# A two-pass channel-attention kernel: the last loads and the maxima back at one width, the first reload cut into six pieces and taken from its last rows, the reloads issued in written order

## The chip, the cores and the metric

The kernel runs on one core of a Trainium2 chip. The metric is the device time of one execution in microseconds.

## The reference

`x` is an image of 384 x 384 positions with 384 channels in bf16 (113 MB), `w1` is 384 x 96 and `w2` is 96 x 384. The mean and the maximum of each channel over all positions go through the same two small matrix products; the sum, through a sigmoid, scales each channel of `x`.

```python
xf  = x.reshape(B, H * W, C)
gap = jnp.mean(xf, 1)
gmp = jnp.amax(xf, 1)
h_a = relu(gap @ w1)
h_m = relu(gmp @ w1)
scale = sigmoid(h_a @ w2 + h_m @ w2)
return x * scale[:, None, None, :]
```

No output element can be written before all of `x` has been read once. The data does not fit in on-chip memory, so most of it is read a second time.

## The kernel before, in words

**Rows and blocks.** The 147456 positions are laid on 128 partitions, 1152 "rows" of 384 channels each. A row over all partitions is 98304 bytes. The first 16 rows are copied to PSUM (`kept_ps`) and stay there; the next 10 rows are read into their own place and read again later into `acc`; the other 1126 rows form 26 blocks: block 0 has 26 rows, blocks 1 to 25 have 44. Six buffers of 44 rows (`slots`, called x_79 to x_84 in the profile, slot 0 to slot 5) take them in turn, so that the last six blocks, 20 to 25, sit in slots 0 to 5 when the first pass ends.

**First pass.** Each entry of `loads` is one DMA on SyncE's queue (L167). For each, TensorE adds the rows to the channel sums (L134), and VectorE takes the maximum of `acc` (11 rows) with up to `width` of the entry's rows at a time (L180). `LAST_LOADS` says into how many pieces the last 13 blocks are cut; all earlier blocks are one DMA of 44 rows. Ahead of the last eight loads, `fold` (L157) takes the maximum of `acc`'s rows 8 to 10 into its first three, and from there on the maxima are 8 rows wide (`NARROW`). The last two loads (`SUM_TAIL`) get their sums through other matmuls (L151), after the earlier sums were turned round in `turn_sums` (L145, L146).

**Between the passes.** VectorE folds `acc` from 8 rows to 1 (L157). Behind the first and the last fold, the rows of `acc` that are free are reloaded with `x` (L201). TensorE transposes the one row left (L204), VectorE reduces it (L205), the two products follow (L207, L209), and ScalarE writes the scale (L210).

**Second pass.** `put` multiplies a block's rows in place, piece by piece, on VectorE (L215), and issues one store per piece on ScalarE's queue (L233); `put_acc` (L222) does so with `acc` after the third piece of the first block. `FIRST_STORES` cuts the first three blocks into pieces; later blocks are one piece. `get` issues the reloads of blocks 0 to 19 on SyncE's queue (L244). After two blocks (`LEAD`) have been put, the first two reloads are written into the program, first the one into slot 1, then the one into slot 0, each in two pieces of 22 rows (`FIRST_READS`); from then on one reload of one piece follows each block, into the slot that the block left. The list `order`, to which each reload is appended, gives the order of the later multiplications. At the end the rows kept in PSUM are multiplied into a slot and stored (L274).

**What sets the order.** The kernel writes no semaphores. A scheduler in the compiler takes the program, keeps the data dependences down to the rows concerned, and may order an engine's instructions otherwise than they are written. A reload waits for the stores of the rows that it overwrites. An engine's queue is in order: a DMA that waits holds back the later ones of its queue.

Of the kernel before, what the change touches and what calls it, by code (L numbers as in the profile page):

```python
# [9 lines left out]
ALU = mybir.AluOpType  # L10
# [7 lines left out]
PSUM_ROWS = 16  # L18
ACC_ROWS = 11

LAST_LOADS = ((22, 22),) * 8 + ((6, 19, 19),) + ((11, 11, 11, 11),) * 2 + ((10, 10, 9, 8, 7), (8, 8, 7, 7, 7, 7))

NARROW = (8, 8)

FIRST_STORES = ((1, 2, 3, 4, 4, 6, 8, 8, 8), (8, 8, 9, 9, 10), (10, 12, 22))

FIRST_READS = (2, 2)
LEAD = 2

ACC_STORES_AT = 3  # L30
# [5 lines left out]
def kernel(  # L36
# [7 lines left out]
    nc = tc.nc  # L44
# [5 lines left out]
    A = ACC_ROWS  # L50
# [7 lines left out]
    def rows_of(ap, first, n):  # L58

        return ap[first * P:(first + n) * P, :].rearrange("(p n) c -> p n c", n=n)  # L60
# [10 lines left out]
    while left > 0:  # L71
        n = min(SLOTS[slot], left)
# [29 lines left out]
    acc = consts.tile([P, A, C], BF16)  # L102
# [17 lines left out]
    for i, (first, n, s) in enumerate(blocks):  # L120
        left = n
        for m in LAST_LOADS[i - n_blocks] if i >= n_blocks - len(LAST_LOADS) else (n,):
            m = min(m, left)
# [3 lines left out]
    n_loads = len(loads)  # L127
    tail_rows = sum(hi - lo for *_, lo, hi in loads[n_loads - SUM_TAIL:])

    def sums(rows, n, done, total):  # L130
        for k in range(0, n, MM_ROWS):
            g = min(MM_ROWS, n - k)
            for q in range(CQ):
                nc.tensor.matmul(  # L134
                    sum_ps[q * QP:q * QP + 1, 0:g * P],
                    lhsT=ones_bf[:, 0:1],
                    rhs=rows[:, k:k + g, q * P:(q + 1) * P],
                    start=(done + k == 0),
                    stop=(done + k + g == total),
                )  # L140

    def turn_sums():

        for r in range(MM_ROWS):
            nc.scalar.copy(out=s_sb[r % 2], in_=sum_ps[:, r * P:(r + 1) * P])  # L145
            nc.tensor.matmul(gsum_ps, lhsT=s_sb[r % 2], rhs=pick, start=(r == 0), stop=False)  # L146

    def tail_sums(rows, n, last):
        for k in range(n):
            for q in range(CQ):  # L150
                nc.tensor.matmul(  # L151
                    gsum_ps[:, q:q + 1], lhsT=rows[:, k, q * P:(q + 1) * P], rhs=ones_bf,
                    start=False, stop=(last and k == n - 1 and q == CQ - 1),
                )

    def fold(n, h):
        nc.vector.tensor_tensor(out=acc[:, 0:h, :], in0=acc[:, 0:h, :], in1=acc[:, n - h:n, :], op=ALU.max)  # L157

    done = 0
    width = A  # L160
    for i, (first, n, s, lo, hi) in enumerate(loads):
        if i == n_loads - NARROW[1]:
            fold(A, A - NARROW[0])
            width = NARROW[0]
        rows = slots[s][:, lo:hi, :]
        m = hi - lo
        nc.sync.dma_start(out=rows, in_=rows_of(xr, first, n)[:, lo:hi, :])  # L167
        if i < n_loads - SUM_TAIL:
            sums(rows, m, done, TOT - tail_rows)
        else:  # L170
            tail_sums(rows, m, i == n_loads - 1)
        done += m
        if i == n_loads - SUM_TAIL - 1:
            turn_sums()
        if i == 0:
            nc.vector.tensor_copy(out=acc, in_=rows[:, 0:A, :])  # L176
            lo = A
        for j in range(0 if i else A, m, width):
            k = min(width, m - j)
            nc.vector.tensor_tensor(out=acc[:, 0:k, :], in0=acc[:, 0:k, :], in1=rows[:, j:j + k, :], op=ALU.max)  # L180
        if i == 0:
            nc.vector.tensor_copy(out=kept_ps.bitcast(U32), in_=rows.bitcast(U32))  # L182
# [6 lines left out]
        nc.tensor.matmul(hTa_ps, lhsT=w1_sb[:, q, :], rhs=gT[:, q, 0:1], start=(q == 0), stop=(q == CQ - 1))  # L189
    nc.scalar.activation(out=hid[:, 0:1], in_=hTa_ps, func=ACT.Relu)  # L190
    nc.tensor.matmul(z_ps, lhsT=hid[:, 0:1].to_broadcast([R, P]), rhs=w2_sb, start=True, stop=False)
    n = width
    acc_pieces = []
    while n > 1:
        h = n // 2
        fold(n, h)
        n -= h
        if n > 1 and acc_pieces:
            continue
        lo, hi = n, acc_pieces[0][0] if acc_pieces else A  # L200
        nc.sync.dma_start(out=acc[:, lo:hi, :], in_=rows_of(xr, PSUM_ROWS, A - 1)[:, lo - 1:hi - 1, :])  # L201
        acc_pieces.append((lo, hi))
# [21 lines left out]
    def put(block, pieces, acc_at=None):  # L224

        first, n, s = block
        j = 0
        for i, m in enumerate(pieces):
            if i == acc_at:
                put_acc()  # L230
            rows = slots[s][:, j:j + m, :]
            multiply(rows, rows)
            nc.scalar.dma_start(out=rows_of(orr, first, n)[:, j:j + m, :], in_=rows)  # L233
            j += m
        assert j == n

    def cut(n, parts):
        return [n // parts + (k < n % parts) for k in range(parts)]

    def get(block, pieces):  # L240
        first, n, s = block
        j = 0
        for m in pieces:
            nc.sync.dma_start(out=slots[s][:, j:j + m, :], in_=rows_of(xr, first, n)[:, j:j + m, :])  # L244
            j += m


    order = blocks[n_stream:]
    again = sorted(blocks[:n_stream], key=lambda b: -b[1])
    stores, reads = list(FIRST_STORES), list(FIRST_READS)  # L250

    def read_into(s):
        fits = [b for b in again if b[1] <= SLOTS[s]]
        if fits:
            b = fits[0]
            again.remove(b)
            b = (b[0], b[1], s)
            get(b, cut(b[1], reads.pop(0) if reads else 1))
            order.append(b)

    k = 0
    while k < len(order):
        put(order[k], stores.pop(0) if stores else (order[k][1],), None if k else ACC_STORES_AT)
        k += 1
        if k == LEAD:
            read_into(order[k - 1][2])
            for j in range(k - 1):
                read_into(order[j][2])
        elif k > LEAD:
            read_into(order[k - 1][2])  # L270
    assert not again
    s = order[-NS][2]
    multiply(slots[s][:, 0:PSUM_ROWS, :], kept_ps)
# [29 lines left out]
```

## Time and profile before

| | |
|---|---|
| median of three runs | 746.55 us (746.23 to 748.59) |
| the profiled execution's own time | 748.59 us |
| its span, first to last instruction | 746.8 us |
| VectorE busy | 489.1 us (65%) |
| TensorE busy | 126.5 us (17%) |
| read from HBM, written to it | 199.11 MB, 113.25 MB |
| mean rate over the span | 418 GB/s |

The profiled execution is the slowest of the three and lies 2.0 us over the median; its span lies 1.8 us under its own time. Times inside the execution are given in us from the start of the span. Reads go over the queue q1 (SyncE), stores over q10 (ScalarE); both are served by the same 16 DMA engines. In the slices of the page one digit or number stands for a fortieth of the span, 18.7 us.

### The profile page before, as it was taken

To read this page: it belongs to the slowest core of one execution; us is meant where nothing else is said; L and a number is where in the kernel's file an instruction comes from. 1 tells how busy PE (TensorE), PEld (TensorE's weight loads), DVE (VectorE), ACT (ScalarE), POOL (GpSimd) and SP (SyncE) were. 2 spreads that over 40 slices of the span, in tenths; PEclk is the share of its full clock that TensorE was granted. 3 is DMA by queue.
4 is the path that set the end of the run, shared out by engine and by line. 5 is a ranking of instruction groups with operands and counts; after the bars stand their busy time and mean duration, and the time that the engine had idled before them with its cause. 6 is when DMAs were issued, how large, how long until landed. Compare 5 with 4: busy or idle time off the path is not lost.

```text
span 746.8 us, 2450 instructions
## 1 busy us (share of the span) xinstructions
PE 126.5 (17%) x958; PEld 40.3 (5%) x958; DVE 489.1 (65%) x166; ACT 3.3 (0%) x9; POOL 0.7 (0%) x6
## 2 busy tenths in 40 slices
PE   3344444445545540000000000000000000000000
PEld 0111111111111120000000000000000000000000
DVE  6789999999999989999443333444444444444600
ACT  0000000000000000000000000000000000000000
POOL 0000000000000000000000000000000000000000
PEclk9656666755555555555555555555555555555555
DMA  9999999999999959999999999999999999999996
GB/s 381 433 432 433 430 427 434 419 426 429 426 424 419 416 217 371 416 434 430 434 429 429 434 433 434 434 433 434 434 434 434 431 434 433 433 434 428 438 431 283
DMA packets 17803, 312.52 MB, mean 418 GB/s; under 512 B 2336, under 2 KB 2688, under 8 KB 6528
## 3 DMA queue, kind: packets, MB, share of 16 engines
q1 hardware_dynamic: 11600, 199.12, 62.7%
q10 hardware_dynamic: 6192, 113.25, 35.5%
q8 instruction: 7, 0.11, 0.1%
q14 instruction: 4, 0.03, 0.0%
HBM read 199.11 MB, written 113.25 MB: 418 GB/s over the span
## 4 chain that ended last, share of the span: by engine, by line
another core or an unknown queue 40%; DVE 31%; DMA 21%; DVEq 1%; issue 1%; SPq 1%; PE 0%; ACT 0%; ACTq 0%
DVE acc L180 28%; DMA out_dram<-x_83 7%; DMA x_81<-in_x_dram 6%; DMA x_79<-in_x_dram 4%; DMA out_dram<-x_80 2%; DMA x_80<-in_x_dram 2%; DVE x_79 L215 1%; DVEq L298 1%; SPq L244 1%; DVE x_80 L215 1%; DVE acc L157 0%; DVE acc L215 0%; DVE acc L176 0%; DVE kept_ps L182 0%
## 5 line engine op out<-in xcount | busy, mean ns | idle before, releaser
L215 DVE TENSOR_TENSOR x_80<-x_80,scale_bc 128x16896 bf16<-128x16896 bf16 (+3 forms) x9 | 45.1, 5044 | 34.3 <-DMA x_80<-in_x_dram 34.3
L215 DVE TENSOR_TENSOR x_79<-x_79,scale_bc 128x3072 bf16<-128x3072 bf16 (+7 forms) x13 | 41.8, 3261 | 30.5 <-DMA x_79<-in_x_dram 29.3
L215 DVE TENSOR_TENSOR x_82<-x_82,scale_bc 128x16896 bf16<-128x16896 bf16 x4 | 35.8, 8956 | 33.7 <-DMA x_82<-in_x_dram 33.7
L215 DVE TENSOR_TENSOR x_83<-x_83,scale_bc 128x16896 bf16<-128x16896 bf16 x4 | 35.8, 8957 | 33.6 <-DMA x_83<-in_x_dram 33.6
L215 DVE TENSOR_TENSOR x_84<-x_84,scale_bc 128x16896 bf16<-128x16896 bf16 x4 | 35.8, 8956 | 33.3 <-DMA x_84<-in_x_dram 33.3
L215 DVE TENSOR_TENSOR x_81<-x_81,scale_bc 128x16896 bf16<-128x16896 bf16 (+3 forms) x6 | 36.0, 6021 | 32.7 <-DMA x_81<-in_x_dram 22.0
L180 DVE TENSOR_TENSOR acc<-acc,x_84 128x4224 bf16<-128x4224 bf16 (+2 forms) x22 | 47.5, 2158 | 5.4 <-DMA x_84<-in_x_dram 4.8
L134 PEld LDWEIGHTS <-small 128*1 128x1 bf16 x897 | 36.1, 110 | 230.4 <-issue 227.2
L180 DVE TENSOR_TENSOR acc<-acc,x_83 128x4224 bf16<-128x4224 bf16 (+5 forms) x20 | 43.6, 2178 | 2.2 <-DMA x_83<-in_x_dram 1.6
L180 DVE TENSOR_TENSOR acc<-acc,x_80 128x4224 bf16<-128x4224 bf16 (+3 forms) x18 | 40.0, 2225 | 3.1 <-DMA x_80<-in_x_dram 2.5
L180 DVE TENSOR_TENSOR acc<-acc,x_79 128x4224 bf16<-128x4224 bf16 (+1 forms) x17 | 38.9, 2287 | 1.5 <-DMA x_79<-in_x_dram 1.0
L180 DVE TENSOR_TENSOR acc<-acc,x_81 128x4224 bf16<-128x4224 bf16 x16 | 37.7, 2359 | 1.9 <-DMA x_81<-in_x_dram 1.4
L180 DVE TENSOR_TENSOR acc<-acc,x_82 128x4224 bf16<-128x4224 bf16 x16 | 37.7, 2359 | 1.0 <-DMA x_82<-in_x_dram 0.5
L134 PE MATMUL bank_a<-x_83,small 128*1 128x512 bf16 (+3 forms) x162 | 22.3, 577 | 25.7 <-DMA x_83<-in_x_dram 25.7
L134 PE MATMUL bank_a<-x_79,small 128*1 128x512 bf16 (+1 forms) x150 | 20.6, 585 | 30.2 <-DMA x_79<-in_x_dram 30.2
L134 PE MATMUL bank_a<-x_80,small 128*1 128x512 bf16 (+2 forms) x147 | 20.8, 593 | 23.2 <-DMA x_80<-in_x_dram 23.2
L134 PE MATMUL bank_a<-x_84,small 128*1 128x512 bf16 (+2 forms) x162 | 20.2, 528 | 25.4 <-DMA x_84<-in_x_dram 25.4
L134 PE MATMUL bank_a<-x_82,small 128*1 128x512 bf16 (+2 forms) x138 | 18.9, 576 | 21.7 <-DMA x_82<-in_x_dram 21.7
L134 PE MATMUL bank_a<-x_81,small 128*1 128x512 bf16 (+2 forms) x138 | 18.7, 571 | 20.0 <-DMA x_81<-in_x_dram 20.0
L176 DVE COPY acc<-x_79 128x4224 bf16<-128x4224 bf16 x1 | 1.3, 1260 | 5.5 <-DMA x_79<-in_x_dram 5.5
L182 DVE COPY kept_ps<-x_79 128x3072 uint32<-128x3072 uint32 x1 | 3.4, 3355 | 0.0
L215 DVE TENSOR_TENSOR x_81<-kept_ps,scale_bc 128x6144 bf16<-128x6144 bf16 x1 | 3.4, 3352 | 0.0
(37 smaller groups left out, 21.0 us busy)
## 6 DMA issues: line engine op xcount, KB each, us to landing
x_84<-in_x_dram SPq DMA_DIRECT2D x5, 4224.0 KB, 30.0
x_80<-in_x_dram SPq DMA_DIRECT2D x5, 4224.0 KB, 30.5
x_81<-in_x_dram SPq DMA_DIRECT2D x5, 4224.0 KB, 30.2
x_82<-in_x_dram SPq DMA_DIRECT2D x5, 4224.0 KB, 30.0
x_83<-in_x_dram SPq DMA_DIRECT2D x5, 4224.0 KB, 30.4
x_79<-in_x_dram SPq DMA_DIRECT2D x4, 4224.0 KB, 30.2
out_dram<-x_82 ACTq DMA_DIRECT2D x4, 4224.0 KB, 75.3
out_dram<-x_83 ACTq DMA_DIRECT2D x4, 4224.0 KB, 70.8
```

Of the source, the lines that this page charges most:

```text
L134: nc.tensor.matmul(sum_ps[q * QP:q * QP + 1, 0:g * P], lhsT=ones_bf[:, 0:1], rhs=rows[:, k:k + g, q * P:(q + 1) * P], start=(done + k == 0 ...
L176: nc.vector.tensor_copy(out=acc, in_=rows[:, 0:A, :])
L180: nc.vector.tensor_tensor(out=acc[:, 0:k, :], in0=acc[:, 0:k, :], in1=rows[:, j:j + k, :], op=ALU.max)
L182: nc.vector.tensor_copy(out=kept_ps.bitcast(U32), in_=rows.bitcast(U32))
L215: nc.vector.tensor_tensor(out=dst, in0=src, in1=scale_bc.unsqueeze(1).to_broadcast([P, n, C]), op=ALU.mult)
L244: nc.sync.dma_start(out=slots[s][:, j:j + m, :], in_=rows_of(xr, first, n)[:, j:j + m, :])
L298: with _tile.TileContext(nc) as tc:
```

## The change

Three things change together.

1. The first pass. The last 12 blocks (before: 13) are cut, eight into two loads of 22 rows and four into four of 11. Before, block 21 was cut into 6, 19 and 19 rows, block 24 into five and block 25 into six pieces. `NARROW` and the fold ahead of the last eight loads go; the maxima stay 11 rows wide, and the last folds go from 11 rows (5, 3, 1, 1 rows) instead of from 8 (4, 2, 1).
2. The first reloads. The reload into slot 0 is written ahead of that into slot 1. It is cut into six pieces of 4, 4, 6, 8, 10 and 12 rows instead of two of 22; the one into slot 1 stays at two of 22. `get` now begins with a block's last rows and goes back to its first.
3. The order. All of the second pass stands in a block in which SyncE's instructions are issued as written.

```diff
-LAST_LOADS = ((22, 22),) * 8 + ((6, 19, 19),) + ((11, 11, 11, 11),) * 2 + ((10, 10, 9, 8, 7), (8, 8, 7, 7, 7, 7))
-
-NARROW = (8, 8)
+LAST_LOADS = ((22, 22),) * 8 + ((11, 11, 11, 11),) * 4
...
-FIRST_READS = (2, 2)
+FIRST_READS = ((4, 4, 6, 8, 10, 12), (22, 22))
...
-        if i == n_loads - NARROW[1]:
-            fold(A, A - NARROW[0])
-            width = NARROW[0]
...
-        for j in range(0 if i else A, m, width):
-            k = min(width, m - j)
+        for j in range(0 if i else A, m, A):
+            k = min(A, m - j)
...
-    n = width
+    n = A
...
     def get(block, pieces):
         first, n, s = block
-        j = 0
+        j = n
         for m in pieces:
+            j -= m
             nc.sync.dma_start(out=slots[s][:, j:j + m, :], in_=rows_of(xr, first, n)[:, j:j + m, :])
-            j += m
+        assert j == 0
...
-            get(b, cut(b[1], reads.pop(0) if reads else 1))
+            get(b, reads.pop(0) if reads else (b[1],))
             order.append(b)
...
+    in_order = ctx.enter_context(ExitStack())
+    in_order.enter_context(tc.manual_schedule(engines={mybir.EngineType.SP}))
     k = 0
     while k < len(order):
...
         if k == LEAD:
-            read_into(order[k - 1][2])
-            for j in range(k - 1):
+            for j in range(k):
                 read_into(order[j][2])
         elif k > LEAD:
             read_into(order[k - 1][2])
+    in_order.close()
```

More of the change, by code (lines that the diff above doesn't have):

```diff
@@ L154, in tail_sums @@
                 )
-    def fold(n, h):
-        nc.vector.tensor_tensor(out=acc[:, 0:h, :], in0=acc[:, 0:h, :], in1=acc[:, n - h:n, :], op=ALU.max)
     done = 0
-    width = A
     for i, (first, n, s, lo, hi) in enumerate(loads):
-        if i == n_loads - NARROW[1]:
-            fold(A, A - NARROW[0])
-            width = NARROW[0]
         rows = slots[s][:, lo:hi, :]
@@ L195 @@
         h = n // 2
-        fold(n, h)
+        nc.vector.tensor_tensor(out=acc[:, 0:h, :], in0=acc[:, 0:h, :], in1=acc[:, n - h:n, :], op=ALU.max)
         n -= h
@@ L235, in put @@
         assert j == n
-    def cut(n, parts):
-        return [n // parts + (k < n % parts) for k in range(parts)]
     def get(block, pieces):
         first, n, s = block
-        j = 0
+        j = n
         for m in pieces:
+            j -= m
             nc.sync.dma_start(out=slots[s][:, j:j + m, :], in_=rows_of(xr, first, n)[:, j:j + m, :])
-            j += m
+        assert j == 0
     order = blocks[n_stream:]
```

## The prediction

> **What bounds the kernel now.** First the page's slices, to see which resource is full where.
>
> ```profile
> DVE  6789999999999989999443333444444444444600
> DMA  9999999999999959999999999999999999999996
> GB/s 381 433 432 433 430 427 434 419 426 429 426 424 419 416 217 371 416 434 430 434 429 429 434 433 434 434 433 434 434 434 434 431 434 433 433 434 428 438 431 283
> ```
>
> DMA is full except at the start, at slice 15 (261 to 280 us), where the first pass ends and the scale is made, and in the last slice. After 400 us VectorE is busy for 134.37 of 300 us and the rate is a flat 433 GB/s. So the time is the bytes over that rate, plus three holes. The change touches the middle hole and the DMAs just behind it.
>
> What makes the middle hole shows in the timeline (start, us, engine, line, tile).
>
> ```profile
> 137.45 4.75 DVE L180 TENSOR_TENSOR acc<-acc,x_83 128x4224 bf16<-128x4224 bf16 x2 [0.50 <-DMA x_83<-in_x_dram]
> ...
> 263.08 9.92 DVE L180 TENSOR_TENSOR acc<-acc,x_84 128x3072 bf16<-128x3072 bf16 x6
> 273.04 1.95 DVE L157 TENSOR_TENSOR acc<-acc 128x1536 bf16<-128x1536 bf16 x3
> ...
> 290.21 9.81 SPq L244 DMA_DIRECT2D x_79<-in_x_dram  x2
> ...
> 312.59 5.29 SPq L244 DMA_DIRECT2D x_80<-in_x_dram  x2
> ```
>
> VectorE last waits for a load at 137.45, for block 12, which comes as one DMA of 44 rows. From there to 275.00 it runs without a gap. The loads' last packets end by 270 (the window 268 to 270 moved 73 GB/s), so VectorE, not the load, opens the hole. TensorE is through with the averages at 272.47, 2.5 us before it is needed. The same view shows SyncE issuing x_79's reload ahead of x_80's although the program has them the other way: the scheduler already had that order.
>
> Behind the hole I asked for the busy time by stretch (last columns: DMA share, GB/s).
>
> ```profile
> 282.00:290.00 8.00, 0.00 (x0) 0.00 (x0) 8.00 (x7) 0.00 (x0) 0.00 (x0) 0.50 1.02 407
> 290.00:300.00 10.00, 0.00 (x0) 0.00 (x0) 10.00 (x6) 0.00 (x0) 0.00 (x0) 0.50 1.00 356
> 300.00:312.00 12.00, 0.00 (x0) 0.00 (x0) 12.00 (x4) 0.00 (x0) 0.00 (x0) 0.50 1.01 426
> 740.00:746.80 6.80, 0.00 (x0) 0.00 (x0) 0.00 (x0) 0.00 (x0) 0.00 (x0) 0.50 0.15 64
> ```
>
> While x_79's first reload mixes with the first block's last stores the engines are busy but move 356 GB/s: against 433 that loses 10 x (1 - 356/433) = 1.8 us. And at the end 6.8 us move 0.44 MB, 1.0 us of work: the 16 engines finish unevenly, and 5.8 us go to waiting for the last.
>
> **What the Trainium skill says.** "DMA: Bandwidth & Descriptors", Queues, rings and completion order: SyncE and ScalarE own a ring each on the same 16 engines, which take turns between them by packets. The trace agrees: from 600 to 700 us q1 had 46.2% and q10 53.8% of the time. Same page, Anatomy of one DMA: about 2 us of a DMA are fixed, mostly the receipt at the end; here a 96 KB store took 1.7 us to landing. Same page, Where 436 GB/s comes from: a ceiling of 435 GB/s; here 433. "VectorE: DVE Perf Modes", Mode 2x_1P: two bf16 results a cycle, so 384 elements at its 0.96 GHz are 200 ns, an estimate. The groups by form say 2358 ns for 4224 elements and 359 for 384: 200 a row, and 159 fixed.
>
> **The change part by part.**
>
> *Start of the chain.* Block 13 becomes one load. VectorE ended block 12 at 147.02 and took block 13's first half at once; now it waits for the whole block. Whole blocks came 10.03 apart (waits that end at 107.36 and 137.45), so 137.45 + 10.03 = 147.48: **+0.46**.
>
> *The maxima.* Before, from 147.02 to 273.04: 126.02, with pieces of 6 to 10 rows and one extra fold. After: 13 blocks of four 11-row maxima, 9.57 a block (127.41 and 137.0 bracket one): 124.41, **-1.61**. The maxima end at 271.89.
>
> *Does the last load hold them up?* Matmuls on 11-row pieces start 2.57 apart (233.57, 236.14, 238.70). Block 21 ends at 228.44; sixteen pieces more give 228.44 + 41.1 = 269.5. The last maximum wants to start at 271.89 - 2.39 = 269.50. A tie: I take 0; if the loads are late, this gain shrinks.
>
> *The folds.* Before 4, 2, 1 rows: 0.96 + 0.56 + 0.36 with gaps, 1.96. After 5, 3, 1, 1: 1.16 + 0.76 + 0.36 + 0.36 + gaps = 2.70: **+0.74**. So `acc` is down to one row at 274.59 instead of 275.00: **-0.41** for the scale and all behind it, since transposes to sigmoid (275.04 to 277.93) stay.
>
> *Hidden there.* The last two loads have 22 rows instead of 14: 66 tail matmuls for 42, at 30 ns (1.26 us for 42) 0.7 us. TensorE's chain then ends near 269.5 + 1.0 + 1.7 = 272.2, under the folds' end by 2.4. `turn_sums` and the two weight loads on SyncE come earlier, since the third last load does. `acc` reloads 5 + 5 rows for 7 + 3: the second piece, issued at 274.6, carries 0.2 MB more, 0.5 us, and lands near 278.8; its multiplication starts at about 280.1 (three pieces and five rows after 277.5). Covered by 1.3 us; without the cover, at most 0.5.
>
> *The reload into x_79.* Its first piece now overwrites rows 40 to 43 and waits for that slot's last store, issued at 289.64 - 0.4 = 289.2; its sisters took 4.2 to land: about 293.4, where before the first half went at 290.2 and the second at 299.7. Four more DMAs at 0.33 to 0.42 on SyncE, 1.5 us; behind them in that queue are only x_80's reloads, which wait to about 312 anyway. Cover for the later start: VectorE turns out a row in 0.204 (8.95 us for 44), DMA stores it in 98304 B / 407 GB/s = 0.24, and the first 16 rows of x_80 are issued by 292.6, 3.9 us of work, while the reload's data comes some 2 us after issue. So DMA doesn't run dry. Without the cover: 2 us. Price of small pieces: first-pass loads in small pieces ran at 419 GB/s (220 to 260), 22-row ones at 426; for 4.33 MB that is 0.17, with 4-row pieces a little more: **+0.25**.
>
> *Counters.* The chain of waits has ScalarE's queue held until a reload lands, though it stores other rows:
>
> ```profile
> 312.59 13.13 DMA x_80<-in_x_dram
> 325.72 0.02 issue
> 325.74 0.02 ACTq L233
> 325.76 0.04 issue
> 325.80 48.78 DMA out_dram<-x_83
> ```
>
> In the first pass 22-row loads took 40.4 us to landing and one landed every 5.06: eight in flight. I read both as eight completion counters shared in turn by the two queues. Six small reloads take six of them, so x_80's and x_81's stores queue behind them on ScalarE, and x_79's and x_80's slots come free later. While stores wait, reloads run, and DMA stays full: 0. Bounds below.
>
> *Order.* SyncE had this order, 0. VectorE takes x_79 before x_80: x_79's first halves landed by 311 even before, x_80 was waited for (0.94 at 335.3), and DMA is full then: 0.
>
> Sum: +0.46 - 1.61 + 0.74 + 0.25 = **-0.16 us** against the profiled execution (748.59, span 746.8). That execution lies 2.0 over the median; the sum shifts the median, 746.55, to **746.4 us**. Unknown is what the new mixing does to the 1.8 and the 5.8 us lost: from -1.8 (the loss goes) with up to 2 of the uneven end, to +1.8 (it doubles) with 1 to 2 of uneven end.
>
> **Rivals.**
>
> *A, as summed:* 746.4, with its own range 745 to 748.5.
>
> *B, slower.* Six small reloads and x_80's stores mix at 290 to 310, with stores stalled behind counters. The loss doubles and the engines drift further apart: +1.8 + 1.2 - 0.16 gives 749.4. It decides once the loss near 290 to 310 grows by more than 2.4 us. For it: mixing is where rate was lost. Against: at 300 to 312 reloads also mix with stores of 8 to 12 rows, at 426.
>
> *C, faster.* The reload no longer competes with the first block's last stores, and the 1.8 goes: -0.16 - 1.8, and half a us of the end: 744.1. For it: the loss began with the reload (350 in 290 to 292). Against: the same kind of start happens 3 us later, beside x_80's stores.
>
> *D, the first pass doesn't gain.* The loads come late by over 0.4, or VectorE waits: the folds' +0.74 stands, +0.7 to +1.2: 747.5. Also here: that the order changes nothing, as it was already so.
>
> **How the numbers follow.** 0.3% is 2.2 us, about what a measurement of this kernel can tell from no change. A 0.48, D 0.11, B 0.22, C 0.19. Faster (under 744.3): most of C and a little of A, 0.19. Slower (over 748.8): most of B and a little of A and D, 0.22. The same: 0.59. The range takes in C at its middle and B at its middle: 744.0 to 749.4.
>
> **What would show it.** Right: VectorE's last maximum ends near 271.9, its folds have four instructions and end near 274.6, the first store goes at about 277.9; x_79's first reload is issued near 293.4, all six within 3 us; from 295 to 310 the DMA share stays 1.0. Wrong: a DMA share under 0.9 there, or a rate under 340; the last maximum waiting for a load; the last slice under 270 GB/s or over 310, which would mean that the engines' uneven end decided.

## The result, and the profile after

The changed kernel takes **743.12 us** (median of 6 runs, 742.86 to 743.49), the kernel before beside it 746.38 us (745.30 to 748.59): ratio **0.9955**, 95% interval 0.9941 to 0.9968. It is faster by 0.45%, the forecast was no change, and 743.12 lies 0.9 us under the range. The profiled execution took 743.10 us (span 741.3); that of before took 748.59 and so lies 2.2 us above its own median, which has to be kept in mind wherever the two traces are compared. Two executions in what follows, 757.05 us of e3 and 784.53 us of e8, lie over 1.5% above the fastest of their kernel and are left out of the ratios.

The page's slices of the changed kernel, the same three rows as before:

```profile
DVE  6789999999999989999444444444444444444500
DMA  9999999999999969999999999999999999999998
GB/s 382 430 433 430 426 438 430 421 427 428 426 429 417 420 240 363 410 433 447 427 428 436 436 438 432 430 432 430 436 436 436 432 428 434 430 438 434 432 436 372
```

The holes at the start and in the middle are as they were. The last slice has 372 GB/s where it had 283.

The timeline (start, us, engine, line, tile) for the steps that the prediction timed:

```profile
147.43 4.75 DVE L171 TENSOR_TENSOR acc<-acc,x_84 128x4224 bf16<-128x4224 bf16 x2 [0.50 <-DMA x_84<-in_x_dram]
...
262.31 9.57 DVE L171 TENSOR_TENSOR acc<-acc,x_84 128x4224 bf16<-128x4224 bf16 x4
...
271.91 2.74 DVE L187 TENSOR_TENSOR acc<-acc 128x1920 bf16<-128x1920 bf16 x4
...
278.01 1.48 ACTq L224 DMA_DIRECT2D out_dram<-x_79  x3
...
293.39 5.42 SPq L233 DMA_DIRECT2D x_79<-in_x_dram  x6
```

The maxima end at 271.88, the folds at 274.65 (275.00 before), the first store goes at 278.01 (278.35 before), and the reload into x_79 is issued at 293.39. All of this is as forecast, and together it moves the second pass by 0.34 us only.

Busy time by stretch (last columns: DMA share, GB/s), the same stretches behind the hole, and the end:

```profile
282.00:290.00 8.00, 0.00 (x0) 0.00 (x0) 8.00 (x7) 0.00 (x0) 0.00 (x0) 0.50 1.02 408
290.00:300.00 10.00, 0.00 (x0) 0.00 (x0) 10.00 (x6) 0.00 (x0) 0.00 (x0) 0.50 1.01 360
300.00:312.00 12.00, 0.00 (x0) 0.00 (x0) 12.00 (x4) 0.00 (x0) 0.00 (x0) 0.50 1.02 427
738.00:741.30 3.30, 0.00 (x0) 0.00 (x0) 0.00 (x0) 0.00 (x0) 0.00 (x0) 0.50 0.39 164
```

The loss at 290 to 300 is still there: 360 GB/s, 356 before. What changed is the end. From 738 us on, the changed kernel moved its last 0.54 MB in 3.3 us; the kernel before took 8.8 us for 1.24 MB:

```profile
738.00:746.80 8.80, 0.00 (x0) 0.00 (x0) 0.00 (x0) 0.00 (x0) 0.00 (x0) 0.50 0.33 141
```

If the bytes of each stretch are taken at 433 GB/s, the time left over is what the engines lost there: from 700 us to the end 6.2 us before and 2.7 after; from 280 to 700 us 3.8 and 2.0. The end holds 3.5 of the 5.3 us by which the sums differ.

The end can be seen more closely. The Trainium skill ("DMA: Bandwidth & Descriptors", Why a DMA increments its semaphore by 16 and not by 1) says that each of the 16 engines adds one to the completion count when its share has landed. The trace agrees, and so the counts show how far apart the engines are. Those of the very last store lie **5.6 us** apart before (740.20 to 745.83) and **1.0 us** after (739.38 to 740.39).

So the question for the experiments: which part of the change keeps the 16 engines together?

### The profile page after: what moved, and what is told of

Its sections match the earlier page's. It is cut to its first block, busy times and chain, and to the rows that moved or that the text cites. A ratio compares the mean times of both kernels' runs of the same rounds, so it can differ in the third digit from the quotient of the medians.

```text
span 741.3 us, 2459 instructions
## 1 busy us (share of the span) xinstructions
PE 127.8 (17%) x970; PEld 41.1 (6%) x970; DVE 488.4 (66%) x162; ACT 3.3 (0%) x9; POOL 0.7 (0%) x6
## 4 chain that ended last, share of the span: by engine, by line
another core or an unknown queue 40%; DVE 32%; DMA 20%; DVEq 1%; issue 1%; SPq 1%; PE 0%; ACT 0%; ACTq 0%
DVE acc L171 29%; DMA out_dram<-x_83 6%; DMA x_81<-in_x_dram 6%; DMA x_79<-in_x_dram 3%; DMA x_80<-in_x_dram 3%; DVE x_79 L206 1%; DVEq L290 1%; DVE x_83 L206 1%; DMA out_dram<-x_80 1%; SPq L233 1%; DMA out_dram<-x_79 0%; DVE acc L187 0%; DVE acc L167 0%; DVE acc L206 0%
## 5 line engine op out<-in xcount | busy, mean ns | idle before, releaser
L206 DVE TENSOR_TENSOR x_79<-x_79,scale_bc 128x16896 bf16<-128x16896 bf16 (+6 forms) x13 | 45.4, 3538 | 34.2 <-DMA x_79<-in_x_dram 33.0
L206 DVE TENSOR_TENSOR x_80<-x_80,scale_bc 128x16896 bf16<-128x16896 bf16 (+4 forms) x9 | 41.5, 4643 | 29.1 <-DMA x_80<-in_x_dram 29.1
L206 DVE TENSOR_TENSOR x_81<-x_81,scale_bc 128x16896 bf16<-128x16896 bf16 (+3 forms) x6 | 36.0, 6022 | 29.2 <-DMA x_81<-in_x_dram 22.0
L171 DVE TENSOR_TENSOR acc<-acc,x_84 128x4224 bf16<-128x4224 bf16 x20 | 47.2, 2358 | 5.9 <-DMA x_84<-in_x_dram 5.3
L171 DVE TENSOR_TENSOR acc<-acc,x_83 128x4224 bf16<-128x4224 bf16 (+1 forms) x19 | 43.4, 2285 | 2.1 <-DMA x_83<-in_x_dram 1.6
L171 DVE TENSOR_TENSOR acc<-acc,x_80 128x4224 bf16<-128x4224 bf16 (+1 forms) x17 | 39.9, 2347 | 2.9 <-DMA x_80<-in_x_dram 2.4
L171 DVE TENSOR_TENSOR acc<-acc,x_79 128x4224 bf16<-128x4224 bf16 (+1 forms) x17 | 38.9, 2287 | 1.4 <-DMA x_79<-in_x_dram 1.0
L171 DVE TENSOR_TENSOR acc<-acc,x_81 128x4224 bf16<-128x4224 bf16 x16 | 37.7, 2358 | 1.9 <-DMA x_81<-in_x_dram 1.4
L171 DVE TENSOR_TENSOR acc<-acc,x_82 128x4224 bf16<-128x4224 bf16 x16 | 37.7, 2359 | 1.1 <-DMA x_82<-in_x_dram 0.5
L132 PE MATMUL bank_a<-x_83,small 128*1 128x512 bf16 (+2 forms) x159 | 22.4, 591 | 25.8 <-DMA x_83<-in_x_dram 25.8
L132 PE MATMUL bank_a<-x_84,small 128*1 128x512 bf16 (+2 forms) x153 | 21.3, 592 | 25.7 <-DMA x_84<-in_x_dram 25.7
L132 PE MATMUL bank_a<-x_79,small 128*1 128x512 bf16 (+1 forms) x150 | 19.8, 565 | 27.6 <-DMA x_79<-in_x_dram 27.6
L132 PE MATMUL bank_a<-x_80,small 128*1 128x512 bf16 (+1 forms) x147 | 19.8, 575 | 23.0 <-DMA x_80<-in_x_dram 23.0
L132 PE MATMUL bank_a<-x_82,small 128*1 128x512 bf16 (+2 forms) x138 | 19.3, 586 | 21.3 <-DMA x_82<-in_x_dram 21.3
L132 PE MATMUL bank_a<-x_81,small 128*1 128x512 bf16 (+2 forms) x138 | 19.1, 582 | 20.3 <-DMA x_81<-in_x_dram 20.3
```

Of the source, the lines that this page charges most:

```text
L132: nc.tensor.matmul(sum_ps[q * QP:q * QP + 1, 0:g * P], lhsT=ones_bf[:, 0:1], rhs=rows[:, k:k + g, q * P:(q + 1) * P], start=(done + k == 0 ...
L206: nc.vector.tensor_tensor(out=dst, in0=src, in1=scale_bc.unsqueeze(1).to_broadcast([P, n, C]), op=ALU.mult)
```

## The experiments

All ratios are against the kernel before, run beside. A ratio weighs all executions and not only the median, so a tail of long ones counts: in e2 the medians alone would give 0.9988. "Counts" are the distance between the first and the last of the 16 completion counts of the last store, in the one execution that was profiled. Block 20, which sits in x_79 and is stored first, is called block 79 in some expectations.

### First round: which part

**e1, the first pass alone.** The kernel before with the new `LAST_LOADS`, without `NARROW` and its fold; second pass untouched.

```diff
-LAST_LOADS = ((22, 22),) * 8 + ((6, 19, 19),) + ((11, 11, 11, 11),) * 2 + ((10, 10, 9, 8, 7), (8, 8, 7, 7, 7, 7))
-NARROW = (8, 8)
+LAST_LOADS = ((22, 22),) * 8 + ((11, 11, 11, 11),) * 4
+NARROW = (11, 0)
```

> The kernel before with the first pass of after: the new cut of the last loads, maxima 11 rows wide to the end; reloads and their order as before. Theory (the gain is the 16 DMA engines finishing together, set by the first reload): only the 0.3 to 0.4 us of the earlier scale, so a ratio to before of 0.9995 (0.998 to 1.001), and the last store's 16 completion counts still 3 to 6 us apart. Rival (the first pass makes the gain): ratio 0.9955.

Measured: 742.83 us, **0.9966** (0.9953 to 0.9978), counts 0.6 us. The first pass alone gives the gain, to within the intervals. My first theory after the result, that the new first reload did it, fell.

**e2, the reloads alone.** The first pass of before, the second of the changed kernel.

```diff
-FIRST_READS = (2, 2)
+FIRST_READS = ((4, 4, 6, 8, 10, 12), (22, 22))
 ...
+    in_order.enter_context(tc.manual_schedule(engines={mybir.EngineType.SP}))
```

> The kernel before with the second pass of after: six pieces from the last rows on, reloads in written order, slot 0 first; first pass as before. Theory (uneven end, set by the first reload): nearly the whole gain, ratio 0.996, the last store's completion counts about 1 us apart. Rival (first pass): ratio 0.999 to 1.000.

Measured: 744.87 us, **1.0007** (0.9987 to 1.0028), runs from 744.35 to 753.83; the profiled one is that last, with counts 10.1 us apart. Ten of the 14 lie between 744.3 and 745.5, the other four between 747.1 and 753.8. No gain.

**e3, two halves from the last row on.** The changed kernel with the first reload in two pieces.

```diff
-FIRST_READS = ((4, 4, 6, 8, 10, 12), (22, 22))
+FIRST_READS = ((22, 22), (22, 22))
```

> The kernel after with the first reload in two pieces of 22 rows, still from the last rows on and in written order. If it is the later start that counts (the reload waits for all stores of its block): as after, ratio to before 0.9955. If it is the small pieces that keep the engines in step: back toward before, ratio 0.998 to 1.0, last counts 3 us or more apart.

Measured: 747.17 us, **1.0032** (1.0016 to 1.0048), up to 754.56 among the runs that count, counts 3.5 us. Beside the new first pass, the reload does matter: two halves starting at this moment undo the gain. (A piece of 22 rows moves as 128 packets of 17 KB, one of 8 rows as 128 of 6 KB.)

**e4, the same six pieces from the first row on.**

```diff
-FIRST_READS = ((4, 4, 6, 8, 10, 12), (22, 22))
+FIRST_READS = ((12, 10, 8, 6, 4, 4), (22, 22))
 ...
-        j = n
+        j = 0
         for m in pieces:
-            j -= m
             nc.sync.dma_start(...)
+            j += m
```

> The kernel after with the same six pieces of the first reload, but from the first rows on (12, 10, 8, 6, 4, 4), so that the first piece is issued about 5 us earlier, beside the first block's last stores; x_80's halves from the first rows on too. If the late start counts: back toward before, ratio 0.998 to 1.0. If the small pieces count: as after, 0.9955.

Measured: 743.12 us, **0.9967** (0.9955 to 0.998), counts 1.2 us. Neither the end from which the rows are taken nor the earlier start (the first piece is issued at 286.24, not 293.39) makes a difference beyond the intervals.

**e5, the fixed order alone**, in the kernel before (`manual_schedule` on SyncE, x_79's reload written ahead of x_80's, two halves as before).

```diff
-            read_into(order[k - 1][2])
-            for j in range(k - 1):
+            for j in range(k):
                 read_into(order[j][2])
```

> The kernel before with part 3 of the change alone: the reload into slot 0 written ahead of that into slot 1 and the reloads issued as written; both still in two pieces of 22 rows from the first row on; first pass as before. Since the reloads went in this order before, only VectorE's order of x_79 and x_80 changes: ratio 1.000 (0.999 to 1.001), last counts 3 to 6 us apart as before. Rival: the fixed order itself keeps the engines together, ratio 0.996 to 0.997.

Measured: 745.43 us, **0.9995** (0.9987 to 1.0003), counts 2.5 us. Nothing, as forecast.

### Second round: what in the first pass

Of what the first pass leaves behind, one thing differs that the second pass handles: `acc`'s ten rows are reloaded and stored as 5 and 5, because the folds from 11 rows free rows 6 to 10 first, where those from 8 freed rows 4 to 10.

**e6, only that**: the kernel before, with the first reload of `acc` held to rows 6 to 10.

```diff
-        lo, hi = n, acc_pieces[0][0] if acc_pieces else A
+        lo, hi = (n if acc_pieces else 6), acc_pieces[0][0] if acc_pieces else A
```

> The kernel before with one thing of the new first pass: acc reloaded and stored in 5 + 5 rows instead of 7 + 3, so that its first store goes some 0.7 us earlier and the stores are ahead of the first reload. Theory (the new first pass helps through how the first stores and the first reload meet behind it): ratio to before 0.997, the last counts within 1.5 us, a narrow spread of runs. Rival (the maxima or the state in which the loads leave the engines decide): ratio 1.000 and a spread of runs as before.

Measured: 743.18 us, **0.9965** (0.9953 to 0.9976), counts 0.6 us. This one line gives the gain, to within the intervals.

**e7, the reverse**: e1 with `acc` back at 7 and 3.

```diff
-        if n > 1 and acc_pieces:
+        if n > 1 and (acc_pieces or n > 4):
             continue
-        lo, hi = n, acc_pieces[0][0] if acc_pieces else A
+        lo, hi = (n if acc_pieces else 4), acc_pieces[0][0] if acc_pieces else A
```

> The kernel of the run with the first pass alone (e1), with acc's reload put back to 7 + 3 rows (the first piece now behind the second fold, 0.8 us later). Theory of the meeting of stores and reload: the gain is lost, ratio 0.999 to 1.000 and runs spread over 3 us. Rival: as e1, 0.9966, within 1.5 us.

Measured: 744.87 us, **0.9993** (0.998 to 1.0006), up to 751.63. The gain goes with it, though by the medians 1.1 of the 2.8 us of e6 stay. The profiled execution, one of the quick ones (744.06), has counts of only 1.3 us.

**e8, earlier smaller loads** in the changed kernel, to see whether the hole can be shortened further.

```diff
-LAST_LOADS = ((22, 22),) * 8 + ((11, 11, 11, 11),) * 4
+LAST_LOADS = ((22, 22),) * 11 + ((11, 11, 11, 11),) * 3 + ((11, 11, 11, 6, 5),)
```

> The kernel after with three more blocks cut into halves and the very last load of 11 rows cut into 6 and 5, to get at the hole between the passes. The chain of maxima then starts three blocks earlier (-1.4 us) and ends when the last 5 rows are in: maxima end near 270.9 instead of 271.9, the first store near 277.0. If the engines stay together: ratio to before 0.9955 (0.9967 for after in this series, less 0.9 us). If this, too, shifts how stores and reload meet: up to 1.000 with a wide spread.

Measured: 742.98 us, **0.9959** (0.9946 to 0.9972; four runs). The first store went at 277.98, no earlier: VectorE reached the last block sooner, but now waited 0.23 us for a load at 266.90. Here the loads hold the maxima up, so cutting them earlier does not shorten the hole.

### Third round: why 5 and 5

My theory then was lag: VectorE takes 1.47 us for 7 rows, DMA runs out of stores meanwhile, and all later stores are 0.3 to 0.4 us late when the reload starts.

**e9, the 7 and 3 rows one piece later**, so that a 4-row store covers the gap. Edit in the kernel before: `ACC_STORES_AT = 3` becomes `4`.

> The kernel before, its accumulator still reloaded and stored as 7 and 3 rows, but the two stores put one piece later (after the first four pieces of block 79 instead of the first three), so that a 4-row piece is in the queue while VectorE multiplies the 7 rows. If the gap after the third store is what puts the stores behind (lag theory): no window near 281 to 282 us as low as the 131 GB/s of before, ninth store of block 79 landed by about 296 us instead of 299.6, last store's 16 completion counts within 1.5 us, ratio about 0.9965. If the split into 5 and 5 as such makes the gain (another size of descriptor, another reload): as before, ratio 0.999 to 1.001, counts 2 to 6 us apart.

Measured: 746.04 us, **1.0009** (0.9994 to 1.0024), counts 3.6 us. Part of the gap only moved (282 to 284 us: 318 GB/s, the bytes of each packet spread over its time), so alone this decides little.

**e10, an earlier reload with the split kept**: e6 with the first reload cut 20 and 24, so that it waits for one store less.

```diff
-FIRST_READS = (2, 2)
+FIRST_READS = ((22, 22), (20, 24))
```

> The 5 and 5 split in the kernel before, and block 79's first reload cut 20 and 24 rows instead of 22 and 22, so that it waits for the sixth store of the block and not for the seventh: issued near 288.4 us instead of 290.2, while two 8-row stores are still to be written. Lag theory: what counts is how much of the first block's stores is left when the long read packets begin, so the gain goes: ratio 0.999 to 1.001, the tenth or eleventh store's counts 4 us or more apart. Rival (the gain comes from the first stores having no gap, whatever the reads do): ratio stays at 0.9965, counts within 1 us.

Measured: 744.94 us, **0.9998** (0.9982 to 1.0014), up to 750.8. The gain goes although the split is there, and the stores are as in e6. But the sign for engines out of step did not come: in the profiled execution (744.21) the tenth and the eleventh store have counts 1.2 and 0.7 us apart, where 4 or more was expected, and the last 1.3.

**e11, e2 with the split** (the line of e6 added).

> The first pass of before and the second pass of after (the second experiment), with the accumulator reloaded and stored as 5 and 5 rows. If the split is the whole of the gain: ratio 0.996, last store's counts within 1.2 us. If the new first pass gives something of its own beside it: ratio 0.997 to 0.998. If small pieces need something else to be in step: as the second experiment, 1.000.

Measured: 743.19 us, **0.9968** (0.9956 to 0.998), counts 1.6 us. With the second pass of the changed kernel too, the split makes the gain.

**e12, a later start**: e6 with the first three stores made two.

```diff
-FIRST_STORES = ((1, 2, 3, 4, 4, 6, 8, 8, 8), ...
-ACC_STORES_AT = 3
+FIRST_STORES = ((3, 3, 4, 4, 6, 8, 8, 8), ...
+ACC_STORES_AT = 2
```

> The 5 and 5 split in the kernel before, with the first three stores of 1, 2 and 3 rows made two of 3 rows. The first store then starts after 1.0 us of multiplication instead of 0.3 us, so near 279.1 us instead of 278.4; the bytes and the later stores are the same. Lag theory: the stores are behind by 0.5 to 0.7 us, more than the 0.4 us of before, so the gain goes, ratio 0.999 to 1.001, ninth store landed at 298 us or later, counts 3 us or more apart. Rival (the 7-row store itself does it): the start costs its 0.7 us at most, ratio 0.9965 to 0.9975, last counts within 1.5 us.

Measured: 743.03 us, **0.9966** (0.9953 to 0.9979), counts 1.8 us. The lag theory falls: on most engines e12's store of x_79's rows 20 to 27 is written at the same moment as e9's (middle count 289.95 and 289.94), yet e12 has the gain and e9 does not. What differs is the reload: it is issued at 290.65 against 290.15, and its packets then take 3.6 us to begin against 2.8. The issue is explained: in e12 **one** engine is 0.65 us behind the middle one in that store, and the reload waits for all 16. In e9 none is over 0.1 behind. The longer delay is not explained.

That led to the theory that the last round tests: what counts is how much of block 20 is still unwritten when the reload's 17 KB packets begin.

### Last round: the moment of the reload

**e13 and e14, 7 and 3 rows kept, the reload later.** Only the cuts of block 20's last three stores change; the reload waits for the one with row 22, so for 30 or 32 written rows instead of 28.

```diff
-FIRST_STORES = ((1, 2, 3, 4, 4, 6, 8, 8, 8), ...
+FIRST_STORES = ((1, 2, 3, 4, 4, 6, 10, 7, 7), ...     # e13; e14: 12, 6, 6
```

> The kernel before with its 7 and 3 rows, only the last three stores of block 79 cut 10, 7 and 7 rows instead of 8, 8 and 8. The first reload waits for the store that holds row 22, so it is issued when 30 rows are written instead of 28: about 0.45 us later against the stores, as the late engine makes it in the 5 and 5 kernels. Timing theory (what counts is how much of block 79 is still unwritten on most engines when the long read packets begin): the gain is had without any split, ratio 0.9965 to 0.998, reads alone for a us or two near 294 to 296 us, last store's counts within 2 us. If the 7 and 3 rows do it in another way: ratio 0.999 to 1.001, counts 2 to 6 us apart.

> The same with 12, 6 and 6 rows: the first reload is issued when 32 rows are written, about 0.9 us later than before against the stores. Timing theory: gain as with 30 rows or more surely, ratio 0.996 to 0.9975; the reads may by now begin within the first store of block 80 instead, as in the third experiment, and then it is lost again. If the 7 and 3 rows do it in another way: 0.999 to 1.001.

Measured: e13 744.64 us, **0.998** (0.9971 to 0.999), counts 1.2 us; e14 743.94 us, **0.9971** (0.996 to 0.9982), runs within 1.0 us. A gain without the split, and by the medians a larger one with the later reload. e14 is the firm one of the two; e13's interval overlaps that of e15 below.

**e15, the split kept, the reload earlier**: e6 with `6, 9, 9`, so at 26 rows.

> The 5 and 5 split with block 79's last three stores cut 6, 9 and 9 rows: the first reload is issued when 26 rows are written instead of 28, 0.45 us earlier against the stores, about where the kernel before has it with its 7 and 3. Timing theory: the gain is lost though the split is there, ratio 0.999 to 1.001. If the split as such does it: ratio 0.9965.

Measured: 745.08 us, **0.9992** (0.9978 to 1.0007), up to 750.69, counts 3.4 us. No gain with the split. All three went as the moment demands, and against the split as such. They change the size of block 20's last two stores along with the moment; e10 is free of that, for it leaves every store as it is and only lets the reload wait for an earlier one.

The kernels with a first reload of two long pieces from the first row on, from their traces. "Middle" and "last" are the 8th-9th and the 16th count of the store that the reload waits for; "read" is the start of the eighth read packet, "rows" how many rows had begun to be written by then (the first 44 are block 20, what is above is block 21). Each line is one execution, while the ratio is of all.

```
kernel    middle    last   issue    read   rows   ratio
e10       287.88  288.31  288.36  291.80   34.3   0.9998
e15       288.93  289.35  289.47  291.74   37.2   0.9992
before    290.00  290.10  290.21  292.71   38.4   1
e5        289.86  289.96  290.08  292.62   38.5   0.9995
e9        289.94  290.04  290.15  292.98   38.8   1.0009
e7        289.59  289.68  289.89  293.23   40.9   0.9993
e6        289.71  290.04  290.16  293.87   43.9   0.9965
e1        289.01  289.38  289.59  293.27   44.0   0.9966
e13       290.52  290.64  290.76  294.37   44.0   0.9980
e12       289.95  290.60  290.65  294.27   43.7   0.9966
e14       291.12  291.22  291.34  294.97   46.1   0.9971
```

Up to 40.9 rows there is no gain, from 43.7 on there is. Most of the distance arises after the issue: when the reload was issued, 31.0 rows had begun before and 31.9 in e6. But e6's packets took 3.7 us to begin, those of before 2.5. So the delay alone parts the kernels as well as the rows do (at most 3.4 us without the gain, at least 3.6 with it), and what sets it is not shown.

How the two queues then share the engines is seen in the DMA view of 294 to 296 us (q1: SyncE's reads, q10: ScalarE's stores; packets, MB, share of the 16 engines). The kernel before:

```profile
q1 hardware_dynamic: 30, 0.51, 69.8%
q10 hardware_dynamic: 31, 0.19, 22.7%
```

e15:

```profile
q1 hardware_dynamic: 32, 0.54, 68.5%
q10 hardware_dynamic: 32, 0.22, 26.5%
```

e6:

```profile
q1 hardware_dynamic: 43, 0.73, 89.5%
q10 hardware_dynamic: 9, 0.01, 1.6%
```

e13:

```profile
q1 hardware_dynamic: 39, 0.66, 92.0%
q10 hardware_dynamic: 18, 0.03, 7.7%
```

The Trainium skill ("DMA: Bandwidth & Descriptors", Queues, rings and completion order) says that an engine takes turns between queues packet by packet. The first two fences agree: as many store packets as read packets, so each 6 KB of a store goes with 17 KB of a read. There, what is left of block 20's last store crawls: in the kernel before it lands at 299.62, and the second half of the reload, which waits for it, is issued at 299.70. In e6 and e13 the reads have the engines almost alone, since block 20 is written but for a remnant, and block 21's first store, though issued at 291.41 in e6, has hardly begun by 296 (44.0 rows); why it begins so late is not shown. Block 20's last store lands at 296.44 and 295.01, the second half goes at 296.52 and 295.08.

After a crawl the engines are mostly out of step. The second 8-row store of block 21 has its counts 6.6 us apart in the kernel before and 6.7 in e9, against 0.3 in e6; e10's execution, with 0.7, is an exception. Out of step they can stay: the stores of the kernel before have counts 4.8 to 5.9 us apart from 370 us to the end. But they need not: in the changed kernel they lie 2.3 apart around 400 to 670 us and 1.0 after 700. That out-of-step engines come from the crawl is therefore read from the traces, and not forced by an experiment. That the late second half alone does it is excluded by e12, in which one engine's share of the last store came at 300.23 and the second half was issued at 300.31: the other 15 were done by 294.8, and the gain is there.

## Why the prediction was wrong, point by point

- **Start of the chain, maxima, last load, folds: right.** The wait is 0.50 at 147.43 (forecast 147.48), the maxima end at 271.88 (271.89), the last load's matmuls start at 269.47 (269.5) and VectorE does not wait for it, the folds end at 274.65 (274.59). The first store goes at 278.01, 0.34 earlier; -0.41 was forecast.
- **Hidden there: the step that failed.** It asked of the 5 and 5 rows only whether the second reload lands before its multiplication, and costed them at nothing under a cover of 1.3 us. The cover held. The *stores* of the same rows were not counted. e6 has this one edit and measures 0.9965: about 2.6 us at 746, the gain to within the intervals. With it one of the 16 engines stays 0.3 to 0.4 us behind its fellows until the store that the reload waits for (last less middle count of e6 and e1 in the table), so a little more of block 20 is written when the reload is issued, and nearly all of it when the reload's packets begin. Up to the issue this makes 0.9 of the 5.5 rows between e6 and before; the rest comes with the longer delay of the packets, which stays open.
- **The reload into x_79: right in its time** (293.39; forecast 293.4). Six issues took 5.4 us, not 3. SyncE's waits from 298.6 to 306 us show two:

```profile
SPq L233 <- DMA x_79<-in_x_dram: 5.4, 1, 5.4
SPq L233 <- DMA out_dram<-x_80: 1.0, 1, 1.0
```

  The second is inside the six: the last of them went at 298.49, when the store of x_80 that had used the same counter had landed (298.47). The second to fifth issues took 0.63 to 1.36 us instead of 0.33, for which no wait is seen. The first line comes behind the six: from 298.81 to 304.26 SyncE waited for the third of these reloads to land. It cost nothing, since x_80's reload then waited for stores until 312.30.

  The +0.25 for small pieces doesn't show (427 GB/s at 300 to 312, 426 before). The change of reload is worth nothing by itself (e2); beside the split it keeps what two halves at that moment lose (e3).
- **Counters and order: nothing, as forecast.** The counters are as read: in both traces the DMAs of SyncE and ScalarE use eight semaphores between them, and stores of ScalarE go at 299.29 and 300.87, 0.08 us after the reloads that had the same ones landed. e5 is 0.9995; the DMA share stays at 1.01 and 1.02 from 290 to 312.
- **The unknown: mis-sized.** I let the uneven end give at most 2 us, and half a us in rival C. The range ended at the middle of rival C, so it did not even hold the lower end of my own unknown (746.4 less 3.8). The last counts went from 5.6 to 1.0 us apart, and from 700 us on the profiled executions differ by 3.5. The kernel before was profiled in an execution above its median; against the medians the change gives 3.3 us.
- **Rival C came nearest in time (744.1), not in cause.** Its 1.8 us at 290 to 300 did not go (360 GB/s, 356 before). The sign that the prediction named for an uneven end that decides, a last slice over 310 GB/s, came: 372.

**What stays open.** What makes a reload's packets begin late stands first, since most of the 5.5 rows hang on it. With six small pieces (e2, e11, the changed kernel) the reload starts within block 21's stores, and the same reading fits only in part: e11, which has the gain, starts later against the stores (59.8 rows) than e2 (57.2), which has not, but e8 has it although it starts as early as e2 (56.6). Nor does the delay part these: 3.4 us in the changed kernel and 2.8 in e8, 3.1 in e2. Nor is it shown why e4, whose reload starts at 289.16 with 28 rows written, is unharmed; its packets are 9 KB and less. Why engines that are out of step stay so, with an odd slow packet (between 312 and 470 us 40 took over a tenth longer than the median of their size before, 1 after), is not settled. And that the 1.47 us for 7 rows let the late engine catch up is argued from the counts alone (1.0 us apart in the third store of the kernel before, 0.2 in `acc`'s first; in e6 0.6 and 0.8).

No kernel here beats the changed one by more than the intervals: e1, e4, e6, e8, e11, e12 and e14 lie between 0.9959 and 0.9971.

## What to carry to other kernels

Where two queues share DMA engines, look at when a transfer of long packets begins against a short-packet one that something waits for: issuing it 0.5 to 1.1 us later (e12 against e9, e14 against before) was worth 2 to 3 us of a 746 us kernel here. When an edit changes the size of a piece, count its store as well as its load. And read the spread of the 16 completion counts early and late in the trace: the wide spread at the end of the kernel before is there from 370 us on.

## What the runs showed of the hardware

- The 16 DMA engines can finish one store 5.6 us apart (10.1 us in e2's profile). The kernels with nearly the whole gain also repeat better: runs within 0.6 to 2.2 us of each other (e1, e4, e6, e11, e12, e14; 5 or 6 runs each), against 2.2 to 9.9 us in the others (e2, e3, e5, e7, e9, e10, e13, e15; 13 to 22 runs, which widens them somewhat).
- A reload's packets do not begin a fixed time after its issue: 1.0 us when nothing else moved (the first of `acc`'s in the kernel before, 274.03 to 275.02), and behind the stores 2.3 to 3.4 us in the kernels without the gain of the table, 3.6 to 3.7 in the others. Why isn't known.
- About a microsecond ahead of the first read packets the store packets slow down in every kernel, while no read packet moves yet: in the kernel before a 6 KB packet takes 0.46 us instead of 0.23 from 291.5 on, and the first read packet starts at 292.59. With each packet's bytes spread over its time, the rate falls from 410 to between 200 and 260 GB/s for a microsecond (238 at 292 to 293 us before, 211 at 293 to 294 in e6) and recovers with the reads. This is the loss at 290 to 300 that the prediction saw; nothing tried here removed it.
